# Lightning attention and a SiLU feed-forward on one core: the first product of the fifth token block goes three quarters instead of one half in seven products, block states may be rated on ScalarE, and the pieces of w_in are loaded in another order

## The chip, the cores and the metric

The kernel runs on one core of a Trainium2 chip. The time is the device time of one execution in microseconds (us). TensorE is called PE, VectorE DVE, ScalarE ACT, GpSimd POOL, SyncE SP. PEld is PE's loading of weights, which runs beside its matmuls.

## The reference

Two steps. Linear attention with decay over q, k, v of shape (4, 8, 768, 64), in blocks of 64 positions with a state kv of 64 x 64 per batch and head:

```python
for b in range(nb):
    intra = einsum(einsum(qb, kb) * Dmask, vb)
    inter = einsum(qb * lam_pow, kv_state)
    out[:, :, sl] = intra + inter
    kv_state = lam_block * kv_state + einsum(kb * rev_pow, vb)
```

Then the result, as 3072 tokens of 512 features, goes through `h = x @ w_in` (512 to 2048), `g = h * sigmoid(h)` and `g @ w_out` (2048 to 512). Inputs and outputs are float32; the kernel multiplies in bf16 and adds in float32.

## The kernel before

The work is cut into units: 128 positions of one batch. There are six blocks n of 128 positions and four batches, so 24 units. Two units make a set, for the attention. Sets s0 to s3 hold blocks 0 and 1 of one batch each (the paired sets: `prepare_2`, `first_2`, `second_2`); sets s4 to s11 hold one block of two batches (`prepare`, `first_part`, `second_part`, `after_first`, `after_second`). For the feed-forward, units form groups: groups 0 to 3 are the first four sets (two units, 256 columns), groups 4 to 7 are blocks 2 to 5 (four units, 512 columns).

For a set, q, k and v come by SP's loads (raw); DVE or ACT casts and rates them (kq, vd); q and k are turned, by PE (L559, L746) or, from s6, by a transposing load on SP (L755, kqT). PE makes scores (st_ps, L790) and states (d_ps, L780); DVE masks the scores (st, L854) and adds up the states (yf, y). The carried state is y times the decay of a block (xf, L895, by DVE), copied to bf16 (xe). With st, vd and xe PE makes the attention's output x_ps, which is copied to xt, turned so that features lie on partitions.

The first product `h_ps` = w_in x xt is `product1` (L941): for each 128 of the 2048 features four matmuls (L958), as wide as the group, then a silu on ACT (L973) into g. Group 7, and parts 0 and 1 of group 6 (block 4), go by `product1_spared` (L1040) instead: a two-by-two split of the matrices in seven products instead of eight. One "part" is 512 of the 2048 features (two times 256, 1024 apart); its seven products are 28 matmuls of 256 columns (L1079), where the plain way takes 16 of 512. It needs sums of w_in's quarters (wsum, L1020) and of xt's (xsum), both by DVE, and the partial results go through copies (h_ps<-h_ps and m, by ACT or DVE) and adds (h, DVE) before the silus (L1103). `MIXED` lists the parts of block 4's group that go this way, the plain way keeps the rest (L1274 to L1278).

The second product o_ps is `product2_plain` (L983, matmul L996) for the first four units, and from then on `product2` (L1147, matmul L1209) for four units at a time, in the same seven products, with sums s of g and wsum of w_out (`sums_of_w_out`, L1128). Results go by osb to the output.

Nobody writes the order of instructions out by hand. A `Planner` (L39) is given each piece of work as a task: a key (roughly when it is due, in units), the engines that may run it with a cost each, the tasks that it depends on, and the buffers that it needs out of pools of fixed size. It then simulates the core with these costs and a model of the loads. Whenever an engine is free it takes the ready task with the lowest key whose buffers are to be had, unless another engine that may run it would end sooner. The order that comes out is the program. So an edit to a key, a cost or a pool moves instructions elsewhere too. While PE would be idle early on, the planner puts in fillers (L1291, small matmuls with no use for the result).

The constants that the change touches: `LEAD` (L516) is how many units ahead of its use a set of block 2 or later is keyed. `SEQUENCE` (L248) is the order of the first loads: s for a set's q, k, v on SP's queue, i for a piece of w_in (512 of its 2048 columns) and o for one of w_out, both on POOL's queue; a and b are the two halves of a piece, and a name without them is the whole piece in one load; what stands behind an @ is waited for first. For groups 0 and 1 a tile of `h_ps` is two tasks, one for each half of the piece, if these came by two loads (L965). The pool `one` bounds how many tiles of `h_ps` are under way in plain products (a split tile takes none). `HOLD` (L1195) lets the first `product2` begin with half of the pool `two`, whose other members the plain units hold. `LAZY` (L620) delays the key of the carried state of blocks 0 and 1. `ON` (L1141) is the key of w_out's sums.

The lines that run the first product:

```python
left = [j for j in range(4) if j not in MIXED]
if left:
    product1(len(groups) - 2, [m for j in left for m in (2 * j, 2 * j + 8)])
if MIXED:
    product1_spared(len(groups) - 2, *made, MIXED)
product1_spared(len(groups) - 1, *made, range(4))
```

Of the kernel before, what the change touches and what calls it, by code (L numbers as in the profile page):

```python
# [8 lines left out]
F32 = mybir.dt.float32  # L9
BF16 = mybir.dt.bfloat16  # L10
AF = mybir.ActivationFunctionType
AL = mybir.AluOpType
# [26 lines left out]
class Planner:  # L39
# [179 lines left out]
def kernel(  # L219
# [11 lines left out]
    B, H, S, D = q.shape  # L231
# [12 lines left out]
    PAIRED = 2  # L244
    SETS = [[(0, b), (1, b)] for b in range(B)] + [[(n, b), (n, b + 1)] for n in range(PAIRED, NB) for b in (0, 2)]
    GROUPS = SETS[:4] + [[(n, b) for b in range(B)] for n in range(PAIRED, NB)]
    FRESH, TURNED, ALONE, LEAD = 4, 6, 6, 4.25
    SEQUENCE = "s0 s1 i0a@1.1 i0b i1a i1b i2a i2b i3a i3b o0 o1 s2@1.0 o2 o3 s3 s4"  # L248
    POOLS = dict(bank=8, ra=3, rb=6, kq=3, kqT=3, vd=3, st=3, xe=6, xf=3, y=2, yf=2,
                 xt2=2, xt4=2, g=18, s=12, m=3, osb=3, one=3, two=8, att=6, sp=2)  # L250
    BY_POOL, PLAIN = (), 4
    CASTING, SUMS_AFTER, HURRY, SUMS_ON, HOLD, ONTO = 12, 16, 0.0, 9.0, 1, 24
    EARLY, PACE = 1.0, 1.0
    OPEN, FILLED, SCALED = 4, True, (1,)
    QUERIES = (0, 1, 2, 3)
    SCORED, SOON, HALVED = (0, 1), 1, 2
    ON_ACT = ()
    LAZY, FINE, SAFE, EASY, TAIL, SURE = 2.0, True, 1.3, -0.22, 0.9, 1.5
    XE_2, XE_B, XE_P = {"ACT": 0.42, "DVE": 0.35}, 0.1, False
    MIXED, APART, KEPT = (0, 1), 1, "yf"  # L260
    EAGER, CALM, ON = 10.0, 1.0, 0.0
    S3_IN = "rb"

    ctx.enter_context(tc.manual_schedule())
# [95 lines left out]
    def copy(e, o, i):  # L360
        if e == "ACT":
            nc.scalar.activation(o, i, AF.Copy)  # L362
        elif e == "DVE":
            nc.vector.tensor_copy(o, i)  # L364
        else:
            nc.gpsimd.tensor_copy(o, i)

    def tt(e, o, a, b, op):
        (nc.vector if e == "DVE" else nc.gpsimd).tensor_tensor(o, a, b, op=op)  # L369

    def by_act(what, si, a):
        return {"ACT": 1.7} if f"{what}{si}{a}" in ON_ACT else {"DVE": 0.7}
# [307 lines left out]
    def prepare(si):  # L680
        (n, b), (_, b1) = sets[si]
        nb, bs = 2, (b, b1)
        s = key_of(si)
        rs, (lk, lq, lv) = raw[si]
        o = Set()
        infos.append(o)
        o.n, o.bs, o.nb, o.s, o.si = n, bs, nb, s, si
        o.kq, o.kqT, o.vd, o.st = rs[0] if si >= CASTING else Buf("kq"), Buf("kqT"), Buf("vd"), Buf("st")

        o.paired = n < PAIRED  # L690
        if o.paired:
# [12 lines left out]
        def st_of():  # L704
            return tile_of(o.st, [128, 2, nb, NP, 64], BF16, "st")

        o.kq_of, o.kqT_of, o.vd_of, o.st_of = kq_of, kqT_of, vd_of, st_of

        def cast(e, j, i):
            src = rs[i].tile[:, j * H:j * H + H, :]  # L710
            dst = kq_of()[:, i, j].rearrange("p m h d -> p (m h) d")
            if i and e != "DVE":
                for h in range(H):
                    by_rate(e, dst[:, h], src[:, h], lam_q[:, h:h + 1])
            elif i:
                tt(e, dst, src, lam_q[:, :, None].to_broadcast([128, H, 64]), AL.mult)
            else:
                copy(e, dst, src)

        ck = [[add((s - 1.0, i), by_act("q", si, j) if i else {"DVE": 0.45, "ACT": 0.63}, lambda e, j=j, i=i: cast(e, j, i),  # L720
                   deps=(lk, lq)[i], bufs=[rs[i], o.kq]) for i in range(2)] for j in range(nb)]
        if si < CASTING:
            after("k", [t for ts in ck for t in ts])

        def scale_v(e, j):
            if e != "DVE":
                for h in range(H):
                    by_rate(e, vd_of()[:, j, h], rs[2].tile[:, j * H + h], lam_v[:, h:h + 1])
                return
            tt(e, vd_of()[:, j], rs[2].tile[:, j * H:j * H + H, :], lam_v[:, :, None].to_broadcast([128, H, 64]), AL.mult)  # L730

        cv = [add((s - 0.8, 0), by_act("v", si, j), lambda e, j=j: scale_v(e, j),
                  deps=lv, bufs=[rs[2], o.vd]) for j in range(nb)]
        after("v", cv)
        o.cv, o.ck = cv, ck

        o.turned = []
        if si < TURNED:
            for j in range(nb):
                bank = Bank(fills=False)  # L740

                def turn(e, j=j, bank=bank):
                    t = tile_of(bank, [128, 2, NP, U], BF16, "tr")
                    for i in range(2):
                        for m in range(NP):
                            nc.tensor.transpose(t[:, i, m, :], kq_of()[:, i, j, m], ident)  # L746

                tr = add((s - 0.7, j), {"PE": 0.46}, turn, deps=ck[j], bufs=[bank, o.kq])
                for i in range(2):
                    o.turned.append(add((s - 1.0, 2), {"DVE": 0.43, "ACT": 0.6},  # L750
                                        lambda e, j=j, i=i, bank=bank: copy(e, kqT_of()[:, i, j], bank.tile[:, i]),
                                        deps=[tr], prior=o.turned[-1:] if i else [], bufs=[bank, o.kqT]))
        else:
            def dma_turn(e):
                nc.sync.dma_start_transpose(kqT_of().rearrange("p i b m s -> p (i b m) s"),  # L755
                                            kq_of().rearrange("p i b m h d -> p (i b m h d)"))

            o.turned.append(add((-150.0, si), {"SP": 1.4}, dma_turn, deps=[t for ts in ck for t in ts],
                                bufs=[o.kq, o.kqT], nbytes=0.393 * nb, kind=TURN, late=2.0))
# [87 lines left out]
    def after_first(o, t):  # L847
# [44 lines left out]
        def xf_of():  # L892
            return tile_of(xf_n, [128, 2, NP, 64], F32, "xf")[:, b0:b0 + nb]

        tf = add((s - 0.9, 4), {"DVE": dcost}, lambda e: tt(e, xf_of(), y.tile, rate, AL.mult),  # L895
                 deps=[ty], bufs=[y, xf_n])
        xf_t.append(tf)
        xe_t += blocks(xe_n, xf_of, [tf], [xf_n], 5)

# [140 lines left out]
    def product1_spared(gi, wbufs, wdone, parts):  # L1040
# [23 lines left out]
        for jp in parts:  # L1064
# [5 lines left out]
            def bank_of(b):  # L1070
                return tile_of(b, [128, 2, 256], F32, "h_ps")
# [10 lines left out]
                return add((u0 - EARLY + jp * PACE + i / 7, 1), {"PE": 0.44}, mm, deps=deps + done[r] + wdone[w],  # L1082
                           bufs=held + [x, one, two] + ([wbufs[w]] if w in wbufs else []))

            def keep(pool, deps, P=P, bank_of=bank_of):
                b = Buf(pool)
                t = add((u0 - eager, 5), {"ACT": 0.6, "DVE": 0.69}, lambda e: copy(e, tile_of(b, [128, 2, 256], F32, "m"), bank_of(P)),
                        deps=deps, bufs=[b, P])
                return b, t

            narrow = {"22": Buf("vd" if closing else "y"), "12": Buf("st" if closing else "y")}

            def h_of(x, narrow=narrow):
                return tile_of(narrow[x], [128, 2, 256], F32, "h")

            def total_of(x, kept, deps, R=R, bank_of=bank_of, h_of=h_of, narrow=narrow):
                return add((u0 - eager, 5), {"DVE": 0.7}, lambda e: tt(e, h_of(x), bank_of(R), kept.tile, AL.add), deps=deps,
                           bufs=[R, kept, narrow[x]])

            def silu(dst, src, deps, bufs):  # L1100
                def go(e):
# [7 lines left out]
            c1 = add((u0 - eager, 5), {"ACT": 0.6, "DVE": 0.69}, lambda e, P=P, R=R, f=bank_of: copy(e, f(R), f(P)), deps=[m1], bufs=[P, R])  # L1109
            m2 = product(1, R, "A12", "B21", False, [c1])  # L1110
            s11 = silu((low, lo), lambda R=R, f=bank_of: f(R), [m2], [R])
            m6 = product(2, P, "S2", "T2", False, [c1])
            b2, c2 = keep("kqT" if closing else "kq", [m6])
            m5 = product(3, R, "S1", "T1", True, [s11])
            m7 = product(4, P, "S3", "T3", False, [c2])
            b3, c3 = keep("xf" if closing else KEPT, [m7])
            e22 = total_of("22", b3, [m5, c3])
            m4 = product(5, P, "A22", "T4", False, [c3])
            m3 = product(6, R, "S4", "B22", False, [e22])
            e12 = total_of("12", b2, [m3, c2])  # L1120
            s22 = silu((high, hi), lambda h_of=h_of: h_of("22"), [e22], [narrow["22"]])
            s21 = silu((high, lo), lambda P=P, f=bank_of: f(P), [m4], [P])
            s12 = silu((low, hi), lambda h_of=h_of: h_of("12"), [e12], [narrow["12"]])
# [208 lines left out]
```

## Time and profile before

| | |
|---|---|
| three runs, us | 201.06, 202.1, 202.36 (median 202.1) |
| profiled execution, us | 201.32 |
| its span, us | 199.6 |
| granted PE clock, mean | 0.998 |
| busy of the span: PE, DVE, ACT, POOL | 94%, 73%, 61%, 7% |
| L958, 256 and 512 columns, matmuls recorded | 256 and 151 |
| L1079, matmuls | 168 |
| w_in's loads | 8 of 256 KB |
| w_out's loads | 4 of 512 KB |

The profile is one execution. Its span begins and ends a little inside the time that the run reports (1.7 us). A group's line gives the source line, the engine, what it writes and reads, the shape, how many; then the busy time and the mean duration of one instruction in ns; then the idle time of the engine just ahead of them and what ended most of it. Some matmul records are missing from a trace: 160 matmuls of 512 columns are in the program at L958. Times of matmuls overlap at their ends, so the sum of a group is a little over what PE spends on it; the chain of waits counts each stretch once.

### The profile page before, as it was taken

What the parts mean: (1) busy time and instruction counts of PE and PEld (TensorE: products, weight loads), DVE (VectorE), ACT (ScalarE), POOL (GpSimd) and SP (SyncE); (2) the same over time, 40 slices, a digit from 0 to 9 for tenths busy, and PEclk for the clock granted to TensorE, in tenths of its full rate; (3) what the DMA queues carried; (4) which work ended last, traced back from release to release, by engine and by line L of the source; (5) the groups of instructions that cost most, each with busy time, mean ns of one, the idle gap of its engine ahead of it and who ended that gap; (6) DMA issues with size and microseconds to landing.
All of it is one profiled execution on the core that took longest, in us unless ns stands there. A gap on an engine that the chain in (4) does not pass through costs nothing.

```text
span 199.6 us, 6042 instructions
## 1 busy us (share of the span) xinstructions
PE 187.6 (94%) x2607; PEld 143.7 (72%) x2623; DVE 145.6 (73%) x302; ACT 122.3 (61%) x230; POOL 13.2 (7%) x35
## 2 busy tenths in 40 slices
PE   0699999999999998999999999999999999999993
PEld 0588687547777884667778747488887588888882
DVE  7899220279997999949999774999979763837611
ACT  2867767319896846647291574834795849765320
POOL 6086003000000000000000000000000000000000
PEclk9999999999999999999999999999999999999999
DMA  5999999999999999999989999802911001003213
GB/s 154 290 241 194 213 216 217 275 216 246 248 276 211 220 251 166 266 193 219 275 183 218 219 251 184 186 7 72 143 53 56 3 0 53 3 6 104 95 38 131
DMA packets 84894, 32.89 MB, mean 165 GB/s; under 512 B 62852, under 2 KB 84356, under 8 KB 84868
## 3 DMA queue, kind: packets, MB, share of 16 engines
q1 hardware_dynamic: 75074, 22.55, 56.0%
q0 software_dynamic: 4288, 4.20, 12.8%
q10 hardware_dynamic: 5506, 5.77, 8.9%
q8 instruction: 20, 0.33, 0.7%
q14 instruction: 6, 0.05, 0.1%
HBM read 27.26 MB, written 6.29 MB: 168 GB/s over the span
## 4 chain that ended last, share of the span: by engine, by line
PE 79%; DMA 8%; DVE 8%; POOL 1%; SPq 1%; issue 1%; ACT 0%; POOLq 0%
PE o_ps L1209 29%; PE h_ps L958 27%; PE h_ps L1079 9%; PE o_ps L996 6%; DMA w_in_bf<-in_moe_w_in_dram 4%; DMA raw<-in_q_dram 4%; PE x_ps L820 2%; PE d_ps L780 1%; DVE st L369 1%; DVE kq L369 1%; SPq L411 1%; POOL w_in_bf L437 1%; DVE xe L364 1%; PE st_ps L790 1%; PE x_ps L812 1%; PE tr L559 1%
## 5 line engine op out<-in xcount | busy, mean ns | idle before, releaser
L958 PE MATMUL h_ps<-xt,w_in_bf 128*128 128x256 bf16 (+1 forms) x407 | 66.2, 313 | 1.6 <-ACT xe L362 0.6
L958 PEld LDWEIGHTS <-w_in_bf 128*128 128x128 bf16 x416 | 39.3, 98 | 21.8 <-DVE xt L364 1.2
L973 ACT ACTIVATE g<-h_ps 128x512 bf16<-128x512 f32 x72 | 41.6, 596 | 16.8 <-PE h_ps L958 13.4
L1209 PEld LDWEIGHTS <-g 128*128 128x128 bf16 x320 | 31.2, 98 | 4.7
L1209 PEld LDWEIGHTS <-s 128*128 128x128 bf16 x240 | 23.4, 98 | 3.2
L369 DVE TENSOR_TENSOR st<-st_ps,tri 128x512 bf16<-128x512 f32 x32 | 20.3, 682 | 3.9 <-PE st_ps L790 3.9
L369 DVE TENSOR_TENSOR osb<-o_ps,m 128x512 f32<-128x512 f32 (+1 forms) x18 | 10.7, 599 | 15.8 <-ACT m L362 8.0
L362 ACT ACTIVATE m<-o_ps 128x512 f32<-128x512 f32 (+1 forms) x18 | 9.4, 522 | 18.8 <-PE o_ps L1209 18.7
L369 DVE TENSOR_TENSOR kq<-raw,lam_q 128x512 bf16<-128x512 f32 x24 | 15.9, 685 | 5.1 <-DMA raw<-in_q_dram 4.8
L369 DVE TENSOR_TENSOR vd<-raw,lam_v 128x512 bf16<-128x512 f32 x24 | 15.8, 686 | 4.7 <-DMA raw<-in_v_dram 4.6
L1209 PE MATMUL o_ps<-w_out_bf,s 128*128 128x256 bf16 x160 | 19.1, 273 | 0.0
L1209 PE MATMUL o_ps<-wsum,g 128*128 128x256 bf16 x160 | 18.9, 273 | 0.0
L1209 PE MATMUL o_ps<-w_out_bf,g 128*128 128x256 bf16 x160 | 18.6, 273 | 0.0
L362 ACT ACTIVATE xt<-x_ps 128x512 bf16<-128x512 f32 x16 | 9.8, 642 | 9.0 <-PE x_ps L820 6.1
L996 PE MATMUL o_ps<-w_out_bf,g 128*128 128x512 bf16 x57 | 14.1, 380 | 0.6 <-issue 0.3
L369 DVE TENSOR_TENSOR h<-h_ps,m 128x512 f32<-128x512 f32 x12 | 8.3, 690 | 8.0 <-PE h_ps L1079 3.7
L362 ACT ACTIVATE kqT<-tr 128x512 bf16<-128x512 bf16 x20 | 10.8, 595 | 2.3 <-PE tr L559 2.2
L362 ACT ACTIVATE kq<-raw 128x512 bf16<-128x512 f32 x16 | 9.9, 625 | 1.9 <-DMA raw<-in_k_dram 1.9
L1079 PEld LDWEIGHTS <-wsum 128*128 128x128 bf16 x96 | 9.4, 98 | 1.1
L996 PEld LDWEIGHTS <-g 128*128 128x128 bf16 x64 | 5.9, 98 | 5.5
L369 DVE TENSOR_TENSOR s<-g 128x512 bf16<-128x512 bf16 x20 | 8.3, 420 | 2.1 <-ACT g L973 1.4
L1209 PE MATMUL o_ps<-wsum,s 128*128 128x256 bf16 x80 | 9.6, 273 | 0.0
(93 smaller groups left out, 241.4 us busy)
## 6 DMA issues: line engine op xcount, KB each, us to landing
raw<-in_q_dram SPq DMA_DIRECT2D x12, 512.0 KB, 7.2
raw<-in_k_dram SPq DMA_DIRECT2D x12, 512.0 KB, 7.7
raw<-in_v_dram SPq DMA_DIRECT2D x12, 512.0 KB, 8.1
out_dram<-osb ACTq DMA_DIRECT2D x20, 256.0 KB, 3.9
w_in_bf<-in_moe_w_in_dram POOLq DMA_DIRECT2D x8, 256.0 KB, 9.4
w_out_bf<-in_moe_w_out_dram POOLq DMA_DIRECT2D x4, 512.0 KB, 14.5
out_dram<-osb ACTq DMA_DIRECT2D x4, 128.0 KB, 1.7
out_dram<-osb SPq DMA_DIRECT2D x4, 128.0 KB, 1.7
```

Of the source, the lines that this page charges most:

```text
L362: nc.scalar.activation(o, i, AF.Copy)
L364: nc.vector.tensor_copy(o, i)
L369: (nc.vector if e == "DVE" else nc.gpsimd).tensor_tensor(o, a, b, op=op)
L411: nc.sync.dma_start(out=rs[i].tile.rearrange("p h e d -> p h (e d)"), in_=x[i])
L437: nc.gpsimd.dma_start(out=w_in_bf[:, ks, cs], in_=w_in_r[:, ks, cs])
L559: nc.tensor.transpose(t[:, m, a], o.kq_of()[:, i, m, a], ident)
L820: nc.tensor.matmul(x_of(c)[:, j, m, :], lhsT=o.xe[c].tile[:, (bs[0] + j) % 2, m, :], rhs=o.kqT_of()[:, 1, j, m, halves[c]], start=False, s ...
L958: nc.tensor.matmul(t[:, j, :], lhsT=w_in_bf[:, ko, 128 * (m1 + j):128 * (m1 + j) + 128], rhs=xt[gi].tile[:, ko, :], start=ko == 0 and (j = ...
L973: nc.scalar.activation(t[:, half * per:half * per + per], bank.tile, AF.Silu)
L996: nc.tensor.matmul(t, lhsT=g.tile[:, j, 128 * gp:128 * gp + 128], rhs=w_out_bf[:, ko, :], start=(ko == 0), stop=(ko == KO - 1))
L1079: nc.tensor.matmul(t[:, j, :], lhsT=W[w]()[:, k2, f:f + 128], rhs=X(r)[:, k2, :], start=first and j == 0 and k2 == 0, stop=True, skip_grou ...
L1209: nc.tensor.matmul(t[:, i_, :], lhsT=src(j)[:, k2, 128 * r:128 * r + 128], rhs=W[w]()[:, 2 * j + k2, :], start=first and i_ == 0 and j == ...
```

## The change

Three of block 4's four parts go in seven products rather than two. The task that rates the carried state of a set (tf) may, for blocks 3 and 4, run on ACT as four activations with a scale for each partition, at a cost of 1.1; the planner chooses. In `SEQUENCE`, w_in's piece 3 comes behind piece 0, in halves, and pieces 1 and 2 come last, each in one load. The pool `one` grows from 3 to 4, `HOLD` goes to 0, `LAZY` to 0.5, `ON` to 2.0, `LEAD` to 4.5. New branches for `SHARED` and `WHOLE` are written, but both lists are empty, so neither is run; `keep` and `total_of` take the bank as an argument for the sake of these.

```diff
-    FRESH, TURNED, ALONE, LEAD = 4, 6, 6, 4.25
-    SEQUENCE = "s0 s1 i0a@1.1 i0b i1a i1b i2a i2b i3a i3b o0 o1 s2@1.0 o2 o3 s3 s4"
+    FRESH, TURNED, ALONE, LEAD = 4, 6, 6, 4.5
+    SEQUENCE = "s0 s1 i0a@1.1 i0b i3a i3b i1 i2 o0 o1 s2@1.0 o2 o3 s3 s4"
-                 xt2=2, xt4=2, g=18, s=12, m=3, osb=3, one=3, two=8, att=6, sp=2)
+                 xt2=2, xt4=2, g=18, s=12, m=3, osb=3, one=4, two=8, att=6, sp=2)
-    CASTING, SUMS_AFTER, HURRY, SUMS_ON, HOLD, ONTO = 12, 16, 0.0, 9.0, 1, 24
+    CASTING, SUMS_AFTER, HURRY, SUMS_ON, HOLD, ONTO = 12, 16, 0.0, 9.0, 0, 24
-    LAZY, FINE, SAFE, EASY, TAIL, SURE = 2.0, True, 1.3, -0.22, 0.9, 1.5
+    LAZY, FINE, SAFE, EASY, TAIL, SURE = 0.5, True, 1.3, -0.22, 0.9, 1.5
-    MIXED, APART, KEPT = (0, 1), 1, "yf"
-    EAGER, CALM, ON = 10.0, 1.0, 0.0
+    MIXED, APART, KEPT = (0, 1, 2), 1, 'yf'
+    EAGER, CALM, ON = 10.0, 1.0, 2.0
+    SHARED = ()
+    WHOLE = ()
+    RATED = (3, 4)
...
-        tf = add((s - 0.9, 4), {"DVE": dcost}, lambda e: tt(e, xf_of(), y.tile, rate, AL.mult),
-                 deps=[ty], bufs=[y, xf_n])
+        def next_states(e):
+            if e == "DVE":
+                tt(e, xf_of(), y.tile, rate, AL.mult)
+                return
+            for m in range(NP):
+                by_rate(e, xf_of()[:, :, m], y.tile[:, :, m], lam_be[:, m:m + 1])
+
+        tf = add((s - 0.9, 4), {"DVE": dcost, **({"ACT": 1.1} if n in RATED else {})}, next_states, deps=[ty], bufs=[y, xf_n])
```

The program that comes out differs as follows. PE: 16 matmuls of 512 columns fewer at L958, 28 of 256 columns more at L1079, four more fillers; 24 matmuls of h_ps instead of 28 stand ahead of the first one that needs the second half of the second piece in the sequence (i1b before, i3b after); in the first `product2` the order of bursts of h_ps and o_ps differs. DVE: two adds h more, two xf fewer, five copies taken over from ACT (two kq, one each of kqT, m and osb) and two xe copies given to it. ACT: four silus of L973 and four of L1103 change places, three copies of h_ps more, eight activations of 128 x 128 elements for xf. POOL: w_in's loads are four of 256 KB and two of 512 KB. SP: one turn of q and k (s8) and one load of v (s9) change places.

More of the change, by code (lines that the diff above doesn't have):

```diff
@@ L730, in scale_v, with scale_pair @@
             tt(e, vd_of()[:, j], rs[2].tile[:, j * H:j * H + H, :], lam_v[:, :, None].to_broadcast([128, H, 64]), AL.mult)
-        cv = [add((s - 0.8, 0), by_act("v", si, j), lambda e, j=j: scale_v(e, j),
-                  deps=lv, bufs=[rs[2], o.vd]) for j in range(nb)]
+        def scale_pair(e, m):
+            dst = vd_of()[:, :, 2 * m:2 * m + 2]
+            src = rs[2].tile.rearrange("p (b h) d -> p b h d", h=H)[:, :, 2 * m:2 * m + 2]
+            if e == "DVE":
+                tt(e, dst, src, lam_v[:, None, 2 * m:2 * m + 2, None].to_broadcast([128, nb, 2, 64]), AL.mult)
+                return
+            for h in range(2):
+                by_rate(e, dst[:, :, h], src[:, :, h], lam_v[:, 2 * m + h:2 * m + h + 1])
+        if si in WHOLE:
+            cv = [add((s - 0.8, 0), {"ACT": 0.64, "DVE": 0.42}, lambda e, m=m: scale_pair(e, m), deps=lv, bufs=[rs[2], o.vd]) for m in range(NP)]
+        else:
+            cv = [add((s - 0.8, 0), by_act("v", si, j), lambda e, j=j: scale_v(e, j),
+                      deps=lv, bufs=[rs[2], o.vd]) for j in range(nb)]
         after("v", cv)
@@ L893, in xf_of @@
             return tile_of(xf_n, [128, 2, NP, 64], F32, "xf")[:, b0:b0 + nb]
-        tf = add((s - 0.9, 4), {"DVE": dcost}, lambda e: tt(e, xf_of(), y.tile, rate, AL.mult),
-                 deps=[ty], bufs=[y, xf_n])
+        def next_states(e):
+            if e == "DVE":
+                tt(e, xf_of(), y.tile, rate, AL.mult)
+                return
+            for m in range(NP):
+                by_rate(e, xf_of()[:, :, m], y.tile[:, :, m], lam_be[:, m:m + 1])
+        tf = add((s - 0.9, 4), {"DVE": dcost, **({"ACT": 1.1} if n in RATED else {})}, next_states, deps=[ty], bufs=[y, xf_n])
         xf_t.append(tf)
@@ L1083, in product, with keep, total_of @@
                            bufs=held + [x, one, two] + ([wbufs[w]] if w in wbufs else []))
-            def keep(pool, deps, P=P, bank_of=bank_of):
+            def keep(pool, deps, bank, bank_of=bank_of):
                 b = Buf(pool)
-                t = add((u0 - eager, 5), {"ACT": 0.6, "DVE": 0.69}, lambda e: copy(e, tile_of(b, [128, 2, 256], F32, "m"), bank_of(P)),
-                        deps=deps, bufs=[b, P])
+                t = add((u0 - eager, 5), {"ACT": 0.6, "DVE": 0.69}, lambda e: copy(e, tile_of(b, [128, 2, 256], F32, "m"), bank_of(bank)),
+                        deps=deps, bufs=[b, bank])
                 return b, t
-            narrow = {"22": Buf("vd" if closing else "y"), "12": Buf("st" if closing else "y")}
+            narrow = {"22": Buf("vd" if closing else "y")}
+            if gi not in SHARED:
+                narrow["12"] = Buf("st" if closing else "y")
             def h_of(x, narrow=narrow):
                 return tile_of(narrow[x], [128, 2, 256], F32, "h")
-            def total_of(x, kept, deps, R=R, bank_of=bank_of, h_of=h_of, narrow=narrow):
-                return add((u0 - eager, 5), {"DVE": 0.7}, lambda e: tt(e, h_of(x), bank_of(R), kept.tile, AL.add), deps=deps,
-                           bufs=[R, kept, narrow[x]])
+            def total_of(x, kept, deps, bank, bank_of=bank_of, h_of=h_of, narrow=narrow):
+                return add((u0 - eager, 5), {"DVE": 0.7}, lambda e: tt(e, h_of(x), bank_of(bank), kept.tile, AL.add), deps=deps,
+                           bufs=[bank, kept, narrow[x]])
             def silu(dst, src, deps, bufs):
@@ L1111, in product1_spared @@
             s11 = silu((low, lo), lambda R=R, f=bank_of: f(R), [m2], [R])
[L1112 to L1123, printed above, removed]
+            if gi in SHARED:
+                m6 = product(2, P, "S2", "T2", False, [c1])
+                m5 = product(3, R, "S1", "T1", True, [s11])
+                b5, c5 = keep(KEPT if not closing else "xf", [m5], R)
+                e4 = add((u0 - eager, 5), {"DVE": 0.7}, lambda e, P=P, R=R, b5=b5, f=bank_of: tt(e, f(R), f(P), b5.tile, AL.add), deps=[m6, c5],
+                         bufs=[P, R, b5])
+                m7 = product(4, P, "S3", "T3", False, [e4])
+                m3 = product(6, R, "S4", "B22", False, [e4])
+                e22 = total_of("22", b5, [m7], P)
+                s22 = silu((high, hi), lambda h_of=h_of: h_of("22"), [e22], [narrow["22"]])
+                m4 = product(5, P, "A22", "T4", False, [e22])
+                s21 = silu((high, lo), lambda P=P, f=bank_of: f(P), [m4], [P])
+                s12 = silu((low, hi), lambda R=R, f=bank_of: f(R), [m3], [R])
+            else:
+                m6 = product(2, P, "S2", "T2", False, [c1])
+                b2, c2 = keep("kqT" if closing else "kq", [m6], P)
+                m5 = product(3, R, "S1", "T1", True, [s11])
+                m7 = product(4, P, "S3", "T3", False, [c2])
+                b3, c3 = keep("xf" if closing else KEPT, [m7], P)
+                e22 = total_of("22", b3, [m5, c3], R)
+                m4 = product(5, P, "A22", "T4", False, [c3])
+                m3 = product(6, R, "S4", "B22", False, [e22])
+                e12 = total_of("12", b2, [m3, c2], R)
+                s22 = silu((high, hi), lambda h_of=h_of: h_of("22"), [e22], [narrow["22"]])
+                s21 = silu((high, lo), lambda P=P, f=bank_of: f(P), [m4], [P])
+                s12 = silu((low, hi), lambda h_of=h_of: h_of("12"), [e12], [narrow["12"]])
```

## The prediction

> **What bounds the kernel now.** I read the busy row and the 40 slices first, then the windows, the chain of waits, PE's own waits, and the groups with forms kept apart.
>
> ```profile
> PE 187.6 (94%) x2607; PEld 143.7 (72%) x2623; DVE 145.6 (73%) x302; ACT 122.3 (61%) x230; POOL 13.2 (7%) x35
> PE   0699999999999998999999999999999999999993
> PEclk9999999999999999999999999999999999999999
> PE 79%; DMA 8%; DVE 8%; POOL 1%; SPq 1%; issue 1%; ACT 0%; POOLq 0%
> ```
> PE is full from the third slice on, at an undiminished clock. So the time is PE's work plus the holes in it. The windows (us, length, then busy time of PE, PEld, DVE, ACT, POOL) show the holes:
>
> ```profile
> 16.90:22.30 5.40, 4.81 (x68) 3.46 (x67) 4.30 (x9) 4.01 (x8) 1.53 (x3) 1.00 1.17 210
> 22.30:60.40 38.10, 37.60 (x473) 27.35 (x478) 21.48 (x40) 25.29 (x48) 1.86 (x3) 1.00 1.17 239
> 60.40:76.60 16.20, 15.58 (x335) 12.76 (x336) 15.21 (x28) 10.67 (x20) 0.00 (x0) 1.00 1.08 226
> 76.60:196.50 119.90, 119.37 (x1487) 91.08 (x1496) 89.97 (x188) 71.55 (x133) 0.00 (x0) 1.00 0.59 125
> ```
> After 22.3 us PE lacks 1.65 us in all (0.50+0.62+0.53). The chain of waits (start, us, what) tells what led into 22.3 and what one matmul costs:
>
> ```profile
> 13.32 8.96 DMA w_in_bf<-in_moe_w_in_dram
> 22.32 3.67 PE h_ps L958 x32
> 75.39 0.61 DVE xf L369
> 76.02 0.64 ACT xe L362
> 91.44 1.73 PE h_ps L958 x8
> 140.88 0.87 PE h_ps L1079 x8
> 147.85 1.75 PE h_ps L1079 x16
> ```
> A landing of w_in at 22.28 is the last thing other than PE until about 61. At 61 to 76 a VectorE chain carries it, ending in PE's one wait of 0.57 us there, and after that PE alone. PE's waits (total, times, longest) agree:
>
> ```profile
> PE h_ps L958 <- ACT xe L362: 0.6, 1, 0.6
> PE h_ps L958 <- DMA w_in_bf<-in_moe_w_in_dram: 0.2, 1, 0.2
> ```
>
> **The change part by part.**
>
> Three parts of four in seven. The order of instructions after the change shows 16 matmuls of 512 columns fewer at L958 and 28 of 256 columns more at L1079. Unit prices from the chain: a wide one 1.75/8 = 0.2187 us, a narrow one 1.75/16 = 0.1093. So -16 x 0.2187 = -3.50, +28 x 0.1093 = +3.06: **-0.44 us of PE**. The other end is the mean of the groups, whose busy time holds the overlapping ends of bursts:
>
> ```profile
> L958 PE MATMUL h_ps<-xt,w_in_bf 128*128 128x512 bf16 x151 | 35.4, 380 | 1.0 <-ACT xe L362 0.6
> L1079 PEld LDWEIGHTS <-wsum 128*128 128x128 bf16 x96 | 9.4, 98 | 1.1
> L369 DVE TENSOR_TENSOR h<-h_ps,m 128x512 f32<-128x512 f32 x12 | 8.3, 690 | 8.0 <-PE h_ps L1079 3.7 <-ACT m L362 3.6 <-ACT g L973 0.5
> L369 DVE TENSOR_TENSOR xf<-y,lam_be 128x512 f32<-128x512 f32 x6 | 4.1, 686 | 0.0
> L362 ACT ACTIVATE xe<-xf 64x256 bf16<-64x256 f32 x7 | 2.9, 414 | 0.1
> ```
> There 16 x 0.234 against 28 x 0.139 (L1079 has 23.3 us in 168) gives +0.15. I take -0.44: in the chain's bursts PE is gapless, and the 98 ns weight load still hides under 109 ns.
>
> The Trainium skill, "TensorE: Matmul & The Clock Gate", section "Back-to-back issue gap", gives a sustained 131 ns for 512 columns and would halve the worth of what is removed; by it the sum would be 28 x 0.109 - 16 x 0.131 = +0.96, an estimate. The trace's 0.2187 disagrees with it, and fits the page's isolated formula; the row decides, and the rule gets no chance.
>
> Beside PE, that part costs VectorE two more adds (h, 2 x 0.69 = 1.38) and ScalarE three copies more (0.6 each); four silus of one kind take the place of four of another. They lie between 150 and 160 us, where the windows show VectorE 8.38 and ScalarE 7.23 us busy of 10: hidden, but the copies feed the next product of the same part, so cover is thin. By walking the new order with the old durations I find slacks of 0.1 to 0.2 us at the copy and silu and 0.45 at the add. Ends 0 and +0.8 (four hand-overs, 0.2 each); I take 0.
>
> States of blocks 3 and 4. Only one of two per block goes to ScalarE: two VectorE multiplications fewer (-1.2 us), eight activations of 128 elements more on ScalarE. The nearest row is 414 ns for 256 elements, 595 to 629 for 512; on that line some 0.3 each, 1.0 to 1.2 for four. ScalarE stood idle 1.87 and 2.57 us waiting in that place (before the xe copies at 138.6 and 135.6). Behind the four wait the xe copies, needed a whole burst later. Price 0; ends -0.3 (VectorE was 15.4 of 17 us busy from 138 to 155) and +0.3 (the burst does wait). The plan also hands VectorE five copies that ScalarE had (two kq, a kqT, an m, an osb: 0.42 to 0.69 each, 2.6 in all) and ScalarE two of VectorE's xe copies; with the adds and the states VectorE ends 2.0 us heavier over the span. None of them lands in the 61 to 76 stretch by the order, so 0; the cost without that cover is the copy's own 0.4 to 0.7.
>
> w_in's pieces. New order: piece 3 in halves, then 1 and 2 whole, so two POOL issues fewer (2 x 0.75 us, off the path; POOL is 7% busy). By PE's order only 24 narrow h_ps matmuls, not 28, stand ahead of the wait on the second half landing at 22.28; four of group 1's go behind it, and four more fillers fill the hole. That is 4 x 0.1093 = **+0.44 us**, as PE is behind the landing from there on. ScalarE's first evacuation is also later (an xe pair, 0.84, ahead of the second xt), which moves the first h_ps from 16.94 to some 17.65, in front of the same landing: 0. Ends 0 (the landing comes earlier) and +0.9 (the 16.94 to 17.65 shift is not covered).
>
> After 22.3: 36 h_ps, then piece 1 must be whole at 22.3 + 36 x 0.1093 = 26.25; the old half 2b, last in this slot, lands by its packets at 25.95. Then 32 h_ps and 8 transposes (0.45): piece 2 is needed at about 30.2; the slot ends at 29.47. The halves came 1.99 us apart (17.53 to 29.47 for six), whole pieces of w_out 3.67 (33.16 to 36.83): the same rate, price 0. Largest spacing of whole pieces in the trace: 36.83 to 42.37, 5.54, when SyncE's loads share the engines; that is the upper end, priced as a rival below.
>
> HOLD, `one`, LEAD, LAZY, ON. They add no instruction. HOLD makes the first four-unit second product wait for all four plain units (L996) to be stored, so 24 h_ps matmuls run first: order alone. ON and LAZY move VectorE's sums and states within 46 to 76 us; VectorE's list for 61 to 76 is nearly the same length and 15.21 of 16.20 us full, so the 0.57 wait stays. Ends -0.57 (gone) and +0.6 (one such VectorE instruction more in the chain). SyncE: one transpose and one load change places; both land over 1.5 us before use: 0. Without that cover, a transpose in the way costs at most the wait of a burst, 0.5.
>
> Sum: -0.44 + 0.44 + 0 = **0.0 us**. The profiled execution took 201.32 (span 199.6 and 1.7 around it), so 201.3 in its terms. It lies 0.78 under the median, 202.1; the four executions (201.06, 201.32, 202.1, 202.36) have the mean 201.7, and I give that: **201.7 us**.
>
> **The rivals.**
>
> Gain stays. The landing is earlier or the 0.57 wait goes, so the PE saving is kept: 201.7 - 0.44 - 0.57 = 200.7, at most 200.3 with another 0.4. For it: POOL's queue has two issues fewer, and the wait of 0.57 hangs on a VectorE chain that LAZY and ON can reorder. Against: by the order that chain has the same members, and VectorE as a whole gets heavier, not lighter.
>
> Whole pieces late (the other side). Two whole pieces follow each other and PE cannot begin on a half. From 26.25 on each us late is a us lost, since nothing but PE work lies between there and 60. At a spacing of 5.54, piece 1 lands at 27.8 (+1.6 of wait), piece 2 at 33.4 (+1.6 more): 201.7 + 3.2 = 204.9; at half that, 203.3. For it: margins of 0.3 and 0.7 us. Against: SyncE's s2 loads stand behind o1 in the sequence.
>
> ScalarE late in the third part. Its copies, silus and the four rating activations come on an engine that was 4.64 us of 5 busy at 145 to 150. Decides when it is over 0.2 us late at a hand-over: four times 0.2 to 0.4 is +0.8 to +1.6, so 202.5 to 203.3.
>
> The change does not do what it says: SHARED and WHOLE are empty, their code is never run, and half of the states stay on VectorE. The rest is real by the instruction counts. If the planner's new order were all that counts, 201.7 +- 0.6.
>
> **How the numbers follow.** Near even, with that last case: 0.60 (own range 200.8 to 202.6). Gain stays: 0.15. Whole pieces late: 0.12. ScalarE late: 0.13. Leaving out half of the late-piece case and the outer part of the gain, 8 in 10 lie in 200.2 to 203.5. A measurement of this kernel tells 1% (2.0 us) from no change, since its runs span 1.3: faster means under 200.1, slower over 204.1. Faster: half of the gain case and little else, 0.10. Slower: half of the late pieces and a tail of ScalarE's, 0.10. Within: 0.80.
>
> **What would show it.** Right: L958 wide matmuls 0.44 us less in sum with L1079; PE's wait on w_in at about 22 with 24 h_ps ahead; no second wait on w_in; the 0.6 wait on xe near 77; ScalarE's eight rating activations about 0.3 us each. Wrong: a wait on w_in at 26 or 30; PE waits on ScalarE's m or h_ps between 150 and 160; no wait at 77; a landing at other than 22.3; a last matmul that ends far from 196.5.

## The result and the profile after

The changed kernel takes 202.94 us (median of 22 runs, 201.84 to 204.63), the kernel before 201.78 (22 runs, 201.03 to 203.73): the ratio is 1.0056, 95% interval 1.0035 to 1.0076. That is 1.1 us slower. 202.94 lies within 1% and inside the range of 200.2 to 203.5, but above the 200.8 to 202.6 given to the case of no change; no change was the forecast, and the measured one is clear of noise. The profiled execution took 203.24 us, its span 201.5, 1.9 longer than before.

Busy time, the PE slices and the shares of the chain of waits of the kernel after, from the page. (The file is longer, so line numbers have moved: L958, L1079, L1209, L996, L362 and L369 of the kernel before are L980, L1101, L1248, L1018, L365 and L372 here. A q behind an engine's name is its instruction sequencer.)

```profile
PE 187.2 (93%) x2625; PEld 145.1 (72%) x2639; DVE 146.4 (73%) x305; ACT 126.1 (63%) x238; POOL 11.8 (6%) x33
PE   0688699999999998999999999999999999999993
PE 77%; DMA 10%; DVE 8%; POOL 1%; SPq 1%; issue 1%; ACT 1%; DVEq 0%; POOLq 0%
```

PE is busy 0.4 us less, and the span is 1.9 longer. The thinner slices are the third to the fifth, that is 10 to 25 us. The waits of PE (total, times, longest) name what ended them there:

```profile
PE h_ps L980 <- DMA w_in_bf<-in_moe_w_in_dram: 2.0, 2, 1.7
PE h_ps L980 <- ACT xt L365: 0.7, 1, 0.7
PE h_ps L980 <- ACT xe L365: 0.6, 1, 0.6
```

The wait on w_in has gone from 0.2 to 2.0 us. The 0.6 on xe, at 76.6 us before, is still there, at 78.7. PE's order of time (start, us, what, and in brackets the wait ahead), first of the kernel before, then of the one after:

```profile
16.94 1.91 PE L958 MATMUL h_ps<-xt,w_in_bf 128*128 128x256 bf16 x16
19.57 0.61 PE L958 MATMUL h_ps<-xt,w_in_bf 128*128 128x256 bf16 x4
20.50 0.60 PE L958 MATMUL h_ps<-xt,w_in_bf 128*128 128x256 bf16 x4
21.49 0.61 PE L958 MATMUL h_ps<-xt,w_in_bf 128*128 128x256 bf16 x4 [0.17 <-DVE xt L364]
22.32 6.03 PE L958 MATMUL h_ps<-xt,w_in_bf 128*128 128x256 bf16 x52 [0.22 <-DMA w_in_bf<-in_moe_w_in_dram]
```

```profile
18.18 1.91 PE L980 MATMUL h_ps<-xt,w_in_bf 128*128 128x256 bf16 x16 [0.71 <-ACT xt L365]
20.95 0.61 PE L980 MATMUL h_ps<-xt,w_in_bf 128*128 128x256 bf16 x4 [0.29 <-DMA w_in_bf<-in_moe_w_in_dram]
21.62 0.60 PE L980 MATMUL h_ps<-xt,w_in_bf 128*128 128x256 bf16 x4
24.15 6.72 PE L980 MATMUL h_ps<-xt,w_in_bf 128*128 128x256 bf16 x60 [1.70 <-DMA w_in_bf<-in_moe_w_in_dram]
```

The long burst starts at 24.15 instead of 22.32, with 24 matmuls done instead of 28. After that nothing else is lost. With the stretches of the prediction moved along by 1.8 to 2.0 us, the windows of the kernel after (us, length, busy time of PE, PEld, DVE, ACT, POOL) are:

```profile
24.15:62.40 38.25, 37.78 (x475) 27.84 (x480) 21.83 (x41) 25.38 (x47) 1.87 (x3) 1.00 1.14 234
62.40:78.60 16.20, 15.61 (x335) 12.74 (x336) 15.19 (x28) 10.46 (x20) 0.00 (x0) 1.00 1.01 215
78.60:198.30 119.70, 119.23 (x1501) 92.33 (x1508) 90.41 (x191) 75.56 (x142) 0.00 (x0) 1.00 0.59 126
```

PE lacks 0.47, 0.59 and 0.47 us, before it was 0.50, 0.62 and 0.53. So the whole loss of the profiled execution is made by 24.15: the burst starts 1.83 us later, with four matmuls (0.44) still to do that were done by then before; the third part saves some 0.4 later on.

A load is spread over sixteen DMA engines, and the trace records the landing of each one's share. The piece counts as landed when the last share has. Of w_in's second piece and the half in front of it, in us of the span:

| kernel | half ahead: 8th share | first half: 8th | second half: 8th, 15th, last |
|---|---|---|---|
| before (piece 1 behind 0) | 16.67 | 18.73 | 20.61, 21.39, 22.28 |
| after (piece 3 behind 0) | 16.99 | 19.65 | 21.53, 22.31, 24.10 |

Two things are late after. The eighth share, the middle one, is 0.92 later, and it was 0.32 later already at the half ahead; between them the first half took 2.66 instead of 2.06. And the last share came 1.8 behind the fifteenth where it had been 0.9, which is another 0.9. The experiments ask which of these belongs to the change.

### The profile page after: what moved, and what is told of

It is laid out like the page before. It is cut to its first block, busy times and chain, and to the rows that moved or that the text cites. A ratio compares the mean times of both kernels' runs of the same rounds, so it can differ in the third digit from the quotient of the medians.

```text
span 201.5 us, 6084 instructions
## 1 busy us (share of the span) xinstructions
PE 187.2 (93%) x2625; PEld 145.1 (72%) x2639; DVE 146.4 (73%) x305; ACT 126.1 (63%) x238; POOL 11.8 (6%) x33
## 4 chain that ended last, share of the span: by engine, by line
PE 77%; DMA 10%; DVE 8%; POOL 1%; SPq 1%; issue 1%; ACT 1%; DVEq 0%; POOLq 0%
PE o_ps L1248 27%; PE h_ps L980 25%; PE h_ps L1101 11%; PE o_ps L1018 6%; DMA w_in_bf<-in_moe_w_in_dram 5%; DMA raw<-in_q_dram 4%; PE x_ps L836 2%; SPq L414 1%; PE d_ps L796 1%; DVE st L372 1%; DVE kq L372 1%; POOL w_in_bf L440 1%; PE st_ps L806 1%; DVE xe L367 1%; DMA out_dram<-osb 1%; PE x_ps L828 1%
## 5 line engine op out<-in xcount | busy, mean ns | idle before, releaser
L980 PE MATMUL h_ps<-xt,w_in_bf 128*128 128x256 bf16 (+1 forms) x393 | 62.5, 310 | 3.6 <-DMA w_in_bf<-in_moe_w_in_dram 2.0
L980 PEld LDWEIGHTS <-w_in_bf 128*128 128x128 bf16 x400 | 38.1, 98 | 21.5 <-DMA w_in_bf<-in_moe_w_in_dram 2.3
L995 ACT ACTIVATE g<-h_ps 128x512 bf16<-128x512 f32 x68 | 39.5, 597 | 15.7 <-PE h_ps L980 15.4
L1248 PEld LDWEIGHTS <-g 128*128 128x128 bf16 x320 | 31.1, 98 | 4.7
L1248 PEld LDWEIGHTS <-s 128*128 128x128 bf16 x240 | 23.4, 98 | 3.0
L372 DVE TENSOR_TENSOR st<-st_ps,tri 128x512 bf16<-128x512 f32 x32 | 20.5, 681 | 5.1 <-PE st_ps L806 5.1
L372 DVE TENSOR_TENSOR kq<-raw,lam_q 128x512 bf16<-128x512 f32 x24 | 15.7, 681 | 6.4 <-DMA raw<-in_q_dram 6.1
L372 DVE TENSOR_TENSOR vd<-raw,lam_v 128x512 bf16<-128x512 f32 x24 | 15.8, 683 | 5.9 <-DMA raw<-in_v_dram 5.9
L1248 PE MATMUL o_ps<-w_out_bf,s 128*128 128x256 bf16 x160 | 19.1, 273 | 0.0
L1248 PE MATMUL o_ps<-wsum,g 128*128 128x256 bf16 x160 | 18.9, 273 | 0.0
L365 ACT ACTIVATE m<-o_ps 128x512 f32<-128x512 f32 (+1 forms) x17 | 8.8, 517 | 15.7 <-PE o_ps L1248 15.5
L1248 PE MATMUL o_ps<-w_out_bf,g 128*128 128x256 bf16 x160 | 18.5, 273 | 0.0
L372 DVE TENSOR_TENSOR osb<-o_ps,m 128x512 f32<-128x512 f32 (+1 forms) x18 | 10.6, 596 | 9.9 <-ACT m L365 7.1
L372 DVE TENSOR_TENSOR h<-h_ps,m 128x512 f32<-128x512 f32 x14 | 9.6, 689 | 8.8 <-ACT m L365 4.7
L365 ACT ACTIVATE xt<-x_ps 128x512 bf16<-128x512 f32 x16 | 10.0, 640 | 8.6 <-PE x_ps L836 5.3
L1018 PE MATMUL o_ps<-w_out_bf,g 128*128 128x512 bf16 x57 | 14.1, 379 | 0.6 <-issue 0.3
L1101 PEld LDWEIGHTS <-wsum 128*128 128x128 bf16 x112 | 10.9, 98 | 1.5
L365 ACT ACTIVATE kqT<-tr 128x512 bf16<-128x512 bf16 x19 | 10.3, 596 | 2.0 <-PE tr L562 1.6
L1127 ACT ACTIVATE g<-h 128x512 bf16<-128x512 f32 x14 | 8.8, 627 | 3.5 <-DVE h L372 3.2
L1101 PE MATMUL h_ps<-xsum,wsum 128*128 128x256 bf16 x84 | 10.8, 273 | 0.0
L1127 ACT ACTIVATE g<-h_ps 128x512 bf16<-128x512 f32 x14 | 8.3, 595 | 3.1 <-PE h_ps L1101 3.0
L1018 PEld LDWEIGHTS <-g 128*128 128x128 bf16 x64 | 5.9, 98 | 5.5
```

What stands on the lines that cost most here:

```text
L980: nc.tensor.matmul(t[:, j, :], lhsT=w_in_bf[:, ko, 128 * (m1 + j):128 * (m1 + j) + 128], rhs=xt[gi].tile[:, ko, :], start=ko == 0 and (j = ...
L995: nc.scalar.activation(t[:, half * per:half * per + per], bank.tile, AF.Silu)
L1018: nc.tensor.matmul(t, lhsT=g.tile[:, j, 128 * gp:128 * gp + 128], rhs=w_out_bf[:, ko, :], start=(ko == 0), stop=(ko == KO - 1))
L1101: nc.tensor.matmul(t[:, j, :], lhsT=W[w]()[:, k2, f:f + 128], rhs=X(r)[:, k2, :], start=first and j == 0 and k2 == 0, stop=True, skip_grou ...
L1127: nc.scalar.activation(o, src(), AF.Silu)
L1248: nc.tensor.matmul(t[:, i_, :], lhsT=src(j)[:, k2, 128 * r:128 * r + 128], rhs=W[w]()[:, 2 * j + k2, :], start=first and i_ == 0 and j == ...
```

## The experiments

All ratios are to the kernel before on the same chip, with 95% intervals, five rounds each. "Spacing" is the time from the eighth share of the first piece's second half to the eighth share of the next half.

**The old order of pieces.**

```diff
-    SEQUENCE = "s0 s1 i0a@1.1 i0b i3a i3b i1 i2 o0 o1 s2@1.0 o2 o3 s3 s4"
+    SEQUENCE = "s0 s1 i0a@1.1 i0b i1a i1b i2a i2b i3a i3b o0 o1 s2@1.0 o2 o3 s3 s4"
```

> The changed kernel with the old order of w_in's pieces (1, 2, 3 behind 0, all in halves); every other edit stays. In the trace of the changed kernel the second half of the second piece landed at 24.10 us, 1.8 later than before (22.28), and PE waited 1.7 us for it. Theory A (the order or form of the pieces makes that landing late): the landing is back near 22.3, and the time is at or up to 0.5 us under the kernel before: ratio 0.997 to 1.000. Theory B (the landing of the profiled execution was chance, or belongs to the other edits that move SyncE's or PE's early work): the ratio stays near 1.0056. Theory C (the loss is in the third part, HOLD, or the states): the landing may move, but the ratio stays above 1.004.

Measured: 1.0011 (0.9996 to 1.0027). The landing is at 22.79, the spacing 1.92. Theory A holds; B, by which the ratio stays near 1.0056, and C, by which it stays above 1.004, fall: 0.9 us of the loss goes with the order of the pieces alone. The ratio is a little above what A gave (0.997 to 1.000), so something more may cost; PE still waits 0.9 us for w_in, with 24 matmuls done.

**Piece 3 second, but halves.**

```diff
-    SEQUENCE = "s0 s1 i0a@1.1 i0b i3a i3b i1 i2 o0 o1 s2@1.0 o2 o3 s3 s4"
+    SEQUENCE = "s0 s1 i0a@1.1 i0b i3a i3b i1a i1b i2a i2b o0 o1 s2@1.0 o2 o3 s3 s4"
```

> The changed kernel with piece 3 still behind piece 0, but pieces 1 and 2 in halves as before. If the late landing comes from the whole loads queued behind (theory A1), it is back near 22.3 us and the ratio is 0.997 to 1.001. If it comes from which piece is second (theory A2: columns 1536 to 2047 rather than 512 to 1023), the landing stays at 23.5 to 24.1 and the ratio at 1.004 to 1.007.

Measured, in six runs: 1.0061 (1.0040 to 1.0081), spacing 2.76, landing 23.24. The loss is all there with halves, so whole loads are not its cause: A1 falls. My rival of the prediction, "whole pieces late", falls with it.

**The new order on the kernel before.**

```diff
-    SEQUENCE = "s0 s1 i0a@1.1 i0b i1a i1b i2a i2b i3a i3b o0 o1 s2@1.0 o2 o3 s3 s4"
+    SEQUENCE = "s0 s1 i0a@1.1 i0b i3a i3b i1 i2 o0 o1 s2@1.0 o2 o3 s3 s4"
```

> The kernel before with the new order of w_in's pieces alone. Theory A: landing of the second piece at 23.5 to 24.1 us, 24 matmuls ahead of the wait instead of 28, no PE work saved: ratio 1.006 to 1.011. Theory B or C: ratio 1.000 to 1.003 (the four matmuls, 0.44 us, at most).

Measured: 1.0032 (1.0019 to 1.0045), landing 23.15, spacing 2.67. The landing is late as in theory A, but the ratio is far below what A gave and just above B and C. A late landing costs what PE waits for it, and that hangs on the plan. In this plan PE does not wait for the second half: its burst from 22.00 runs on past 23.15. It waits 0.8 us for the first half instead, 0.2 for the whole of piece 1, and, the whole stream being later, 1.0 at w_out:

```profile
PE h_ps L958 <- DMA w_in_bf<-in_moe_w_in_dram: 1.0, 2, 0.8
PE o_ps L996 <- DMA w_out_bf<-in_moe_w_out_dram: 1.0, 1, 1.0
```

**Piece 1 second, in halves; 2 and 3 whole.**

```diff
-    SEQUENCE = "s0 s1 i0a@1.1 i0b i3a i3b i1 i2 o0 o1 s2@1.0 o2 o3 s3 s4"
+    SEQUENCE = "s0 s1 i0a@1.1 i0b i1a i1b i2 i3 o0 o1 s2@1.0 o2 o3 s3 s4"
```

> The changed kernel with piece 1 in halves behind piece 0, then pieces 2 and 3 whole. Theory A1 (whole loads behind make it late): landing of the second piece at 23.5 to 24.1 us, ratio 1.004 to 1.007. Theory A2 (which piece it is): landing near 22.3, ratio 0.997 to 1.001, as in the run with the old order.

Measured: 1.0023 (1.0002 to 1.0044), landing 22.38, spacing 1.78. The landing is as A2 has it, the ratio a little above its end (1.001). PE's wait on w_in is 0.3 us here; a wait of 0.8 at L1248 for nothing that the profile shows is new in this plan. Against halves, whole loads are 0.12% dearer here (1.0023 against 1.0011) and 0.05% cheaper with piece 3 second (1.0056 against 1.0061). The intervals overlap in both, so neither a cost nor a gain of whole loads is shown.

**The old order, and LAZY as before.**

```diff
-    SEQUENCE = "s0 s1 i0a@1.1 i0b i3a i3b i1 i2 o0 o1 s2@1.0 o2 o3 s3 s4"
+    SEQUENCE = "s0 s1 i0a@1.1 i0b i1a i1b i2a i2b i3a i3b o0 o1 s2@1.0 o2 o3 s3 s4"
...
-    LAZY, FINE, SAFE, EASY, TAIL, SURE = 0.5, True, 1.3, -0.22, 0.9, 1.5
+    LAZY, FINE, SAFE, EASY, TAIL, SURE = 2.0, True, 1.3, -0.22, 0.9, 1.5
```

> The changed kernel with the old order of w_in's pieces and LAZY at 2.0 as before, so that ScalarE copies xt ahead of the carried state's xe again and 28 matmuls of h_ps stand ahead of the wait on w_in. My theory: of the run with the old order alone (ratio 1.0011) the rest of the loss was the four matmuls (0.44 us) and the later first h_ps, both through LAZY; then PE's 0.44 us saved in the third part shows: ratio 0.996 to 0.999, PE's wait on w_in 0.2 to 0.6 us instead of 0.9. Rival (the third part saves nothing, its copies cost what it saves): ratio 1.000 to 1.002.

Measured: 0.9991 (0.9975 to 1.0008). The step from 1.0011 is 0.4 us, as expected in size, but the two intervals overlap, so by the times it is not shown. What LAZY does to the order is plain in ScalarE's list of the kernel after, where xe stands between the two xt copies and the first h_ps waits 0.71 us for the second:

```profile
15.75 0.75 ACT L365 ACTIVATE xt<-x_ps 128x512 bf16<-128x512 f32 x1
16.52 0.84 ACT L365 ACTIVATE xe<-xf 64x256 bf16<-64x256 f32 x2
17.39 0.74 ACT L365 ACTIVATE xt<-x_ps 128x512 bf16<-128x512 f32 x1
```

With LAZY at 2.0 the first h_ps starts at 17.14, and 28 matmuls stand ahead of the second half again. (In this execution the half ahead landed at 19.15, which cost PE 1.0 us in the middle of them; in all PE waited 1.3 us for w_in, where 0.2 to 0.6 was expected.)

**Three parts, nothing else.**

```diff
-    MIXED, APART, KEPT = (0, 1), 1, "yf"
+    MIXED, APART, KEPT = (0, 1, 2), 1, "yf"
```

> The kernel before with three parts of block 4 in seven instead of two, nothing else. By PE's rates in the chain of waits -0.44 us: ratio 0.997 to 0.999, no new wait of PE between 140 and 160 us. By the means of the groups (+0.15) or if ScalarE's copies are late (+0.2 to +1): 1.000 to 1.005.

Measured: 0.9991 (0.9965 to 1.0017), and in a second measurement

> The kernel before with three parts of block 4 in seven, once more, to narrow its interval (0.9965 to 1.0017). By PE's rates 0.9978; by the groups' means 1.0007.

0.9995 (0.9976 to 1.0014). Neither tells the saving from nothing. The traces do. In the chain of waits, all from the attention burst of s10 to the last run of o_ps is PE, but for three pieces of 0.05 us in the kernel before. The kernel before, the first and the second of these two runs:

```profile
138.56 0.57 PE x_ps L820 x16
184.26 12.24 PE o_ps L1209 x112
```

```profile
138.48 0.57 PE x_ps L820 x16
183.78 12.24 PE o_ps L1209 x112
```

```profile
139.07 0.57 PE x_ps L820 x16
184.37 12.24 PE o_ps L1209 x112
```

That is 45.70 us before and 45.30 in both: with the third part this stretch is 0.40 us shorter. From 140 to 160 us the windows have PE busy 19.85 us before and 20.00 in both, which looks as if the new order closed holes of 0.15. It did not: the program of the kernel before on other columns of w_in, which is run below (2 then 3), has PE busy 20.00 us of these 20 and takes 45.70 too:

```profile
139.16 0.57 PE x_ps L820 x16
184.86 12.24 PE o_ps L1209 x112
```

So the 0.15 are matmul records missing from the trace of before, and the 0.40 us are PE's own work. All fourteen traces agree: 45.70 in the four with two parts, 45.30 or 45.31 in the ten with three. In the times 0.4 us is less than the intervals can tell, and the start adds a scatter of its own: in the second run the half ahead landed at 18.95, and the burst began late.

**Piece 2 second.**

```diff
-    SEQUENCE = "s0 s1 i0a@1.1 i0b i3a i3b i1 i2 o0 o1 s2@1.0 o2 o3 s3 s4"
+    SEQUENCE = "s0 s1 i0a@1.1 i0b i2a i2b i1a i1b i3a i3b o0 o1 s2@1.0 o2 o3 s3 s4"
```

> The changed kernel with piece 2 behind piece 0, then 1 and 3, all in halves. In the traces so far the middle one of the sixteen shares of the next half landed 1.8 to 2.1 us behind i0b's where piece 1 came next, 2.66 to 2.76 where piece 3 did. If any jump in the columns costs this: again 2.5 or more, ratio 1.003 to 1.007. If it is piece 3 alone: about 1.9, ratio 1.000 to 1.003, as with the old order.

Measured: 1.0034 (1.0014 to 1.0055), spacing 2.79, landing 23.41, a wait of 1.5 us on w_in. Piece 3 is nothing special; with piece 2 second the landing is as late.

**States by VectorE again.**

```diff
-    RATED = (3, 4)
+    RATED = ()
```

> The changed kernel with all states rated by VectorE as before (RATED empty). If the states on ScalarE are free, as I priced them: ratio to the kernel before 1.004 to 1.007, that of the changed kernel. If they are part of the loss: 1.000 to 1.003.

Measured: 1.0042 (1.0021 to 1.0062), landing 23.34, spacing 2.81. That agrees with the states being free. The ratio is 0.3 us under that of the changed kernel; the two intervals overlap and would allow the states some 0.9 us, so the times show neither a cost nor that there is none. In the trace of the kernel after they are four at a time, ahead of the xe copies, and PE has no wait behind them:

```profile
139.58 1.28 ACT L380 ACTIVATE xf<-y,lam_be 128x128 f32<-128x128 f32 x4 [0.67 <-DVE y L372]
140.89 0.63 ACT L365 ACTIVATE xe<-xf 64x512 bf16<-64x512 f32 x1
```

**The same program on other columns.** The kernel before, with the pieces in the order 1, 2, 3, 0 and in the order 2, 3, 0, 1. The plan comes out the same (the instructions of VectorE, ScalarE, GpSimd and SyncE stand in the same order in all three traces); only the columns of w_in that stand in each place differ.

```diff
-    SEQUENCE = "s0 s1 i0a@1.1 i0b i1a i1b i2a i2b i3a i3b o0 o1 s2@1.0 o2 o3 s3 s4"
+    SEQUENCE = "s0 s1 i1a@1.1 i1b i2a i2b i3a i3b i0a i0b o0 o1 s2@1.0 o2 o3 s3 s4"
```

> The kernel before with w_in's pieces in the order 1, 2, 3, 0, all in halves: the same instructions in the same places, other columns. Spacing of the middle share of sixteen from the first piece's second half to the next piece's first half has been 1.74 to 2.07 us for 0 then 1, and 2.66 to 2.81 for 0 then 2 or 3. If neighbouring columns are what makes it short: about 1.9 again, ratio 0.998 to 1.002. If it is that pieces 0 and 1 lie in the same half of w_in's rows: 2.7, PE's wait on w_in longer by up to 0.9 us, ratio 1.002 to 1.005.

```diff
-    SEQUENCE = "s0 s1 i0a@1.1 i0b i1a i1b i2a i2b i3a i3b o0 o1 s2@1.0 o2 o3 s3 s4"
+    SEQUENCE = "s0 s1 i2a@1.1 i2b i3a i3b i0a i0b i1a i1b o0 o1 s2@1.0 o2 o3 s3 s4"
```

> The kernel before with w_in's pieces in the order 2, 3, 0, 1, all in halves. Both accounts (neighbouring columns; the same half of a row) give a short spacing, about 1.9 us, and a ratio of 0.998 to 1.002. A spacing of 2.7 would mean that only 0 then 1 is quick, and a ratio of 1.002 to 1.005.

Measured: 1 then 2: 1.0059 (1.0032 to 1.0085), spacing 2.79, landing 22.99. 2 then 3: 0.9990 (0.9969 to 1.0012), spacing 1.85, landing 22.61. Columns that are neighbours are not enough. What fits all five pairs that were run (0 then 1 and 2 then 3 quick; 0 then 2, 0 then 3 and 1 then 2 slow) is whether the second piece lies in the same half of w_in's rows (columns 0 to 1023 or 1024 to 2047) as the first. Pairs that go back to lower columns were not run as the first two. What is slow is not w_in's queue alone: from 17 to 18.5 us all the DMA engines together moved 130 GB/s with 1 then 2 and 197 with 2 then 3 (the last number of each line):

```profile
17.00:18.50 1.50, 1.48 (x14) 1.32 (x14) 1.50 (x4) 0.83 (x2) 1.29 (x2) 1.00 0.97 130
17.00:18.50 1.50, 1.03 (x8) 0.68 (x7) 1.50 (x4) 0.83 (x2) 0.75 (x1) 1.00 1.16 197
```

With 1 then 2, PE's order of time shows the wait in two places, at the first half and at the second:

```profile
20.02 0.61 PE L958 MATMUL h_ps<-xt,w_in_bf 128*128 128x256 bf16 x4 [0.47 <-DMA w_in_bf<-in_moe_w_in_dram]
23.04 5.85 PE L958 MATMUL h_ps<-xt,w_in_bf 128*128 128x256 bf16 x52 [0.74 <-DMA w_in_bf<-in_moe_w_in_dram]
```

**What stays of the change.**

```diff
-    SEQUENCE = "s0 s1 i0a@1.1 i0b i3a i3b i1 i2 o0 o1 s2@1.0 o2 o3 s3 s4"
+    SEQUENCE = "s0 s1 i0a@1.1 i0b i1a i1b i2a i2b i3a i3b o0 o1 s2@1.0 o2 o3 s3 s4"
...
-    CASTING, SUMS_AFTER, HURRY, SUMS_ON, HOLD, ONTO = 12, 16, 0.0, 9.0, 0, 24
+    CASTING, SUMS_AFTER, HURRY, SUMS_ON, HOLD, ONTO = 12, 16, 0.0, 9.0, 1, 24
...
-    LAZY, FINE, SAFE, EASY, TAIL, SURE = 0.5, True, 1.3, -0.22, 0.9, 1.5
+    LAZY, FINE, SAFE, EASY, TAIL, SURE = 2.0, True, 1.3, -0.22, 0.9, 1.5
```

> The changed kernel with the old order of pieces, LAZY at 2.0 and HOLD at 1: what stays of the change is the third part, the states on ScalarE, ON, LEAD and the pool of four. If those are free and the third part saves its 0.44 us: 0.996 to 0.999. If HOLD was worth something: above the 0.9991 of the run with HOLD at 0.

Measured: 1.0008 (0.9985 to 1.0031), above the expected 0.996 to 0.999. With HOLD at 0 it was 0.9991; the two cannot be told apart. No version that was run is measurably faster than the kernel before.

All fourteen traces together:

| second piece | kernels | spacing, us | second half landed, us |
|---|---|---|---|
| same half of the rows as the first | before and seven others | 1.74 to 2.26, mean 1.95 | 21.50 to 22.87, mean 22.44 |
| other half of the rows | after and five others | 2.66 to 2.81, mean 2.75 | 22.99 to 24.10, mean 23.37 |

The spacings do not overlap; the landings differ by 0.93 us in the mean, which is what the order cost in the times (1.0056 against 1.0011: 0.9 us). The ratios fall apart in the same way: 1.0032 to 1.0061 (mean 1.0047) where the second piece lies in the other half, 0.9990 to 1.0023 (mean 1.0001) in the seven others, which is 0.9 us again, though the kernels differ in other edits too.

## Why the prediction was wrong

The sum was zero because it took the landing of the second half at 22.28 us as belonging to its place in the queue. It is 0.9 us later for the columns that the new order puts there. That is the step that failed: "price 0" for the order of w_in's pieces, with 22.3 taken over for another piece. Two of the signs that the prediction had named came: a landing at other than 22.3, and two waits on w_in where one was expected. The changed kernel has 0.9 us from this, 0.4 from the start, and saves 0.4 in the third part: +0.9, where 1.1 was measured (0.7 to 1.5 by the interval). The profiled execution had the landing 1.8 us later; the half of that which is the last share's lag is this execution's own: the mean landings differ by 0.93 alone.

Point by point:

- **Three parts, -0.44.** Right: 0.40 in every trace with the third part. The means of the groups (+0.15) were wrong for it, as their busy time holds overlapping ends. The Trainium skill's 131 ns for 512 columns ("TensorE: Matmul & The Clock Gate", "Back-to-back issue gap") would have made the part a loss of 0.96, an estimate; the traces show a saving.
- **ScalarE late in the third part.** Did not happen: from 140 to 160 us PE is busy 19.95 us of 20 in the kernel after, and it has no wait on ScalarE or VectorE there.
- **States.** Priced at 0, and no trace shows a wait behind them; the times leave it open. The size was off: 0.39 us each and 1.28 for four, where I had 0.3 and 1.0 to 1.2 on a line through wider copies. The Trainium skill, "ScalarE: Activation LUTs", section "What ACT_TABLE_LOAD costs", gives 186 ns + 0.833 per element, 93 more for a scale for each partition and 93 less where one follows another: 386 ns, and 1.26 us for four, as estimates. The trace agrees.
- **Four matmuls fewer ahead, +0.44.** The count was right, the cause wrong. I put it down to the order of the pieces; with the old order it was still there (24 ahead in that run's order too), and it left with LAZY, which lets ScalarE copy xe ahead of the second half of xt. So it belongs to LAZY. That its size fits all the same is luck.
- **The first h_ps.** I had 17.65; it was 18.18. As priced, it is covered by the landing.
- **Whole pieces late, the rival of the other side.** It named the right wait (w_in, before 27 us) and the wrong reason. With halves the loss is the same, 1.0061; whole loads came 3.63 to 3.70 us apart at the eighth share (mean 3.67), two halves 3.55 to 4.02 (mean 3.72). The Trainium skill's rule to batch loads to 1 MiB or more ("DMA: Bandwidth & Descriptors", "Measured (HBM→SBUF, 128 partitions, SWDGE, issued from GpSimd)") speaks for whole loads; from 256 to 512 KB these runs show 0.05 us of it in the queue and none in the time.
- **The 0.57 us wait near 77 us.** Stayed, as expected: 0.56.
- **VectorE 2.0 us heavier.** It was 0.8 by the page (145.6 to 146.4); nothing hung on it.
- **The holes of 1.65 us after 22.3.** Read as waits, they were too many. In the trace of 2 then 3, the same program, PE is busy all but the 0.57 us wait from 60 to 78 us (17.43 of 18) and the whole time from 100 to 196, so a good part of the 1.65 is missing records.
- **HOLD, `one`, LEAD, ON.** Priced at 0, and no size is shown for them. HOLD at 1 against 0 is 1.0008 against 0.9991. The last run has the other three together with the third part and the states, and its interval is 0.3 us under to 0.6 over the kernel before; with 0.4 saved in the third part, that leaves room for a cost of up to 1 us.

What stays open: why the other half of a row costs 0.8 us in this place and nothing later. No run shows what slows the engines there. In the kernel before the order goes from piece 1 to piece 2 at 20.6 to 22.5 us, and the spacing there is 1.91 like any other. And whether the last share's lag (0.07 to 1.8 us behind the fifteenth) is caused by the fetches of instructions was not tried.

## What to carry to other kernels

Here a landing time belonged to an address as well as to a place in the queue. When an edit puts other data in a slot, the slot's old time is only an estimate, and if PE waits there it needs an upper end of its own. Before a gain of some tenths is forecast, look for the wait nearest the start that all later work hangs on; here 0.9 us there outweighed 0.4 saved by arithmetic. And relabelling which columns stand where, with the program unchanged, is a clean way to test for it.

## What was not expected of the hardware

- **Reads that cross the half of an 8 KB row.** A half piece is 256 rows of 2 KB. Behind the first piece, a piece from the same half of the rows follows at 1.95 us (mean of eight traces), one from the other half at 2.75 (mean of six). From 17 to 18.5 us all engines together moved 121 to 139 GB/s in those six traces; in the eight others 197 to 219, but for one of 152. In 17 to 18.5 us, w_in's packets took 135, 149 and 114 ns in the three half-microseconds of the kernel after, and 102, 98 and 90 of the one before.
- **One of sixteen sets the landing.** The last share of the second half came 0.07 to 1.79 us behind the fifteenth. A 16 KB fetch of instructions goes through the DMA engines at about 13.3 and again at 20 to 21.8 us in every trace, with packets of 0.88 to 1.2 us. It may be what holds the last engine up; this is argued from the times alone. Against it, with three parts alone the fetch came at 20.14 and the last share was 0.35 behind the fifteenth after it, 0.32 in the half ahead of it.
